# Attention with routed experts on one Trainium2 core: softmax weights as the stationary operand, row sums from a column of ones beside v, x kept in f32

## The chip, the core and the metric

The kernel runs on one core of one Trainium2 chip. The metric is the device time of one execution in microseconds (us). The core has a matrix engine (PE, with its weight loads shown apart as PEld), a vector engine (DVE), an activation engine (ACT), a general engine (POOL, GpSimd), a queue engine that issues transfers (SP) and sixteen DMA engines. [...]

## The reference

Rotary attention over 8 batches of 8 heads, 576 positions, 64 values each, then a dense layer plus one of eight experts for each token:

```python
q_rot, k_rot = (rotate(q), rotate(k))
scores = scale * np.matmul(q_rot, k_rot.transpose(0, 1, 3, 2))
scores = scores - np.max(scores, axis=-1, keepdims=True)
attn = np.exp(scores)
attn = attn / (np.sum(attn, axis=-1, keepdims=True) + 1e-09)
return np.matmul(attn, v).astype(np.float32)
...
x = np.ascontiguousarray(attn_out.transpose(0, 2, 1, 3)).reshape(B * S, H * D)   # (4608, 512)
y_dense = np.maximum(x @ w1_dense, 0.0) @ w2_dense
logits = x @ w_gate
expert_idx = np.argmax(logits, axis=1)
gate_w = softmax(logits)[np.arange(N), expert_idx]
y_moe[mask] = gate_w[mask, None] * (np.maximum(x[mask] @ w1[e], 0.0) @ w2[e])    # for each expert e
return (y_dense + y_moe).astype(np.float32)
```

## The kernel before

**Layout.** Two heads at a time (a head pair; 4 pairs in a batch, 32 in all) share tiles. The 576 positions are 512 "main" ones and 64 "tail" ones. Positions stand four by four on the partitions (position 4p+j on partition p, block j), the tail positions on 64 partitions of a fifth block. Nine strips of 128 key positions cover both heads of a pair: 0 to 3 and 5 to 8 are the main strips of the two heads, strip 4 holds both tails.

**One head pair goes through these functions.** `stage_load` brings q and k (f32) by SP's queue into `qk`. `stage_rope` rotates them into `nat` in bf16 (on DVE for the first two pairs, then on POOL). `stage_transpose` turns `nat` into `qkT` by a DMA transpose on SP. `s1_block` multiplies q and k for one strip of queries, and DVE takes the negative row maximum from PSUM (`negm`). `shift_rows` turns the maxima on PE (`mps`), splits them into two bf16 rows (`mT`, ACT and DVE) and copies them by two small SP transfers into spare rows of `qkT`, so that the second pass of scores has the maximum already subtracted. `s2_strip` and `s2_tails` do that second pass with keys on the partitions and take the exponential on ACT into `pm` (main queries) and `pt` (tail queries), in fp16.

**The weighted sums.** `av_mm` multiplies with v, or with a block of ones, as the stationary operand and the probabilities as the moving one; the two heads write to the two halves of the PSUM partitions. `av_sums` gives the row sums of the main queries, repeated on 64 partitions (ACT takes their logarithm, `lz`), `av_tails` the sums and values of the tail queries, `av_main` the values of the main queries. ACT makes the reciprocal as exp(-ln), DVE multiplies into `xf`: values on partitions, tokens along the free axis, f32. After the fourth pair of a batch POOL casts `xf` to `xb` (bf16).

**Logits.** `logits_part` multiplies `xf` with the gate weights in f32 in four column groups of PE at once, ACT copies to `lT`, and `logits_sum` turns that and adds the four groups by a product with `sel` (made once on DVE by `make_sel`). `x_turn` turns `xb` into `natx` (tokens on partitions) by a DMA transpose on SP, and `x_store` writes it as bf16 to the DRAM tensor `xd`.

**V.** `stage_v` loads a batch's v on POOL's queue with a cast to fp16, into one of two buffers `v16`.

**The order of work** is written out by hand: a loop over rounds i (0 to 33) and steps t (0 to 8), which emits at each step one `s1_block` of pair i+2, one `s2_strip` of pair i, and the rest at fixed steps:

```python
if t == 1: av_sums(i - 1)
if t == 4: av_tails(i - 1)
if t == 6: av_main(i - 1)
if t == 2 and i + 1 < NP: shift_rows(i + 1)
if t == 2 and i + LA < NP: stage_rope(i + LA); stage_transpose(i + LA)     # LA = 4
```

At t = 5 come the loads of q or k for later pairs, v of the next batch (in rounds 1, 5, 9, ...) and the expert weights (POOL's queue, rounds 8 to 24). The logits of a batch come in round 5, 9, 13, ..., `x_turn` at the end of rounds 6, 10, ... and `x_store` at the end of rounds 7, 11, .... Each engine and each queue takes its entries strictly in this order. PSUM tiles rotate: two for `s1`, two for `s2` (shared by the second scores, `mps` and the logits), two for `av`.

**Experts.** While the last rounds run, the tokens of the first six batches are planned into tiles of 128 by expert (`gate_steps`, `rank_steps`, `plan_steps`). Then `fetch` gathers each tile's rows of `xd` on POOL's queue (`xg`) and turns them by a DMA transpose (`xs`); `dense_in`, `expert_in`, `expert_turn` and `out_tile` compute a tile, and POOL scatters it to the output.

Of the kernel before, what the change touches and what calls it, by code (L numbers as in the profile page):

```python
# [24 lines left out]
def kernel(  # L25
# [88 lines left out]
    ones = const_p.tile([P, 3, D], fp16)  # L114
    nc.gpsimd.memset(ones, 0.0)
    nc.gpsimd.memset(ones[:, 0, :], 1.0)
    nc.gpsimd.memset(ones[0:64, 1, :], 1.0)
    nc.gpsimd.memset(ones[64:128, 2, :], 1.0)

# [8 lines left out]
    VB = 2  # L130
    v16s = []
    for i in range(VB):
        t = const_p.tile([P, HP, 10, D], fp16, name=f"v16_{i}")
        v16s.append(t)


    GC = 32
    wg_sb = const_p.tile([P, DT, GC], f32)
    nc.gpsimd.memset(wg_sb, 0.0)

    def load_gate():
        nc.sync.dma_start(wg_sb[:, :, 0:E], moe_w_gate.rearrange("(dt p) e -> p dt e", p=P))

    sel = const_p.tile([P, E], f32)

    def make_sel():
        nc.vector.tensor_copy(sel, ident_f[:, 0:E])
        for dt in range(1, DT):
            nc.vector.tensor_tensor(sel, sel, ident_f[:, GC * dt:GC * dt + E], AL.add)

# [4 lines left out]
    XR = DG // 2  # L155
# [20 lines left out]
    def route_constants():  # L176
        nc.gpsimd.iota(first_i, pattern=[[0, 5], [-1, E]], base=E, channel_multiplier=0)
        nc.gpsimd.tensor_copy(first, first_i)
        nc.gpsimd.memset(first[TAIL:P, 4, :], 0.0)
# [15 lines left out]
        nc.gpsimd.iota(tt, pattern=[[S, B], [0, 1]], base=MAIN + 1, channel_multiplier=1)  # L195
# [7 lines left out]
    xb = route_p.tile([P, 5, DT, P], bf16)  # L203
    natx = route_p.tile([P, 5, DG], bf16)
    dram_p = ctx.enter_context(tc.tile_pool(name="xd", bufs=1, space=bass.MemoryType.DRAM))
    xd = dram_p.tile([N, XR], i32)
# [24 lines left out]
    def pad_tails():  # L231

        for t in v16s:
            nc.gpsimd.memset(t[64:128, :, 4, :], 0.0)
            nc.gpsimd.memset(t[0:64, :, 9, :], 0.0)
        nc.gpsimd.memset(xb[:, 4, :, TAIL:P], 0.0)
        nc.gpsimd.memset(lgs, 0.0)
# [17 lines left out]
    def stage_v(b):  # L255
        v16 = v16s[b % VB]
        for a, blk in ((0, 0), (1, 5)):
            heads = v[b, a::2]
            nc.gpsimd.dma_start(v16[:, :, blk:blk + 4, :].rearrange("p h j d -> p h (j d)"),
                                heads[:, 0:MAIN, :].rearrange("h (p j) d -> p h (j d)", j=4))  # L260
            nc.gpsimd.dma_start(v16[64 * a:64 * a + 64, :, blk + 4, :],
                                heads[:, MAIN:S, :].rearrange("h p d -> p h d"))

    def stage_rope(i):
# [4 lines left out]
        if i < 2:  # L269
            a, s = (ap.tile([P, 2, 9, D], bf16, tag="lz", bufs=2, name=n) for n in ("ra", "rb"))  # L270
        else:
            a, s = (early.tile([P, 2, 9, D], bf16, tag=n, bufs=1, name=n) for n in ("ra", "rb"))
# [56 lines left out]
    TAILS = [0, 1, 2, 3, 5, 6, 7, 8, 4]  # L329

    def s2_strip(i, s):
        if s == 0:
            state["pm", i] = ap.tile([P, 9, MAIN], fp16, tag="pm", bufs=2, name="pm")
            state["pt", i] = ap.tile([P, 9, TAIL], fp16, tag="pt", bufs=2, name="pt")
        ps = pp.tile([P, 512], f32, tag="s2", bufs=2, name="s2")
        s2_mm(i, ps, s, False)
        nc.scalar.activation(state["pm", i][:, s], ps, AF.Exp, scale=float(scale))  # L337

    def s2_tails(i, part):
        pt = state["pt", i]  # L340
        n0, n1 = ((0, 8), (8, 9))[part]
        ps = pp.tile([P, 8, TAIL], f32, tag="s2", bufs=2, name="s2")
        for n in range(n0, n1):
            s2_mm(i, ps[:, n - n0], TAILS[n], True)
        nc.scalar.activation(pt[:, n0:n1], ps[:, 0:n1 - n0], AF.Exp, scale=float(scale))

    def av_mm(i, out_ap, tail, sums):

        b, u = divmod(i, HP)
        v16 = v16s[b % VB][:, u]  # L350
        for n in range(5):
            for h in range(2):
                strip = 4 if n == 4 else 5 * h + n
                lhsT = ones[:, 1 + h if n == 4 else 0, :] if sums else v16[:, 5 * h + n, :]
                rhs = state["pt", i][:, TAILS.index(strip)] if tail else state["pm", i][:, strip]
                nc.tensor.matmul(out_ap[64 * h:64 * h + 64], lhsT=lhsT, rhs=rhs, start=(n == 0), stop=(n == 4))  # L356


    def av_sums(i):
        lz = ap.tile([P, S], f32, tag="lz", bufs=2, name="lz")  # L360
        pz = pp.tile([P, 512], f32, tag="av", bufs=2, name="pz")
        av_mm(i, pz, False, True)
        nc.scalar.activation(lz[:, 0:MAIN], pz, AF.Ln)
        state["lz", i] = lz

    def av_tails(i):
        b, hp = divmod(i, HP)
        lz = state.pop(("lz", i))
        px = pp.tile([P, 2, TAIL], f32, tag="av", bufs=2, name="pxt")
        av_mm(i, px[:, 0], True, True)  # L370
        av_mm(i, px[:, 1], True, False)
        nc.scalar.activation(lz[:, MAIN:S], px[:, 0], AF.Ln)
        rz = lz
        nc.scalar.activation(rz, lz, AF.Exp, scale=-1.0)
        if hp == 0:
            state["xf"] = ap.tile([P, DT, S], f32, tag="xf", bufs=2, name="xf")
        nc.vector.tensor_tensor(state["xf"][:, hp, MAIN:S], px[:, 1], rz[:, MAIN:S], AL.mult)  # L377
        state["rz", i] = rz

    def av_main(i):  # L380
        b, hp = divmod(i, HP)
        rz = state.pop(("rz", i))
# [508 lines left out]
```

## Time and profile before

| | |
|---|---|
| median of 3 runs | 591.67 us (591.58 to 594.78) |
| profiled execution | 592.52 us |
| its span, first to last instruction | 590.8 us |
| granted TensorE clock, mean | 0.953 |
| PE busy | 489.3 us (83%) |
| DVE busy | 348.4 us (59%) |
| ACT busy | 295.2 us (50%) |
| POOL busy | 381.8 us (65%) |
| DMA traffic | 83.43 MB, mean 141 GB/s |

Busy times are shares of the whole span, which has stages with different limits; the stages have to be read one by one. PE's matmuls are pipelined, so that their durations overlap: what one costs is read from the start of the next. In a row such as `L326 PE MATMUL s<-qkT`, L326 is the line of the kernel, `s<-qkT` the tile written and the tile read, and after a bar stand idle time and what ended it. "SPq" is SP's queue: the time that issuing a transfer took, not the transfer.

### The profile page before, as it was taken

The numbers are of one execution on the slowest core, as the hardware profiler recorded it, in microseconds if no ns is written. First come the engines' busy times: TensorE is split into PE (matmuls) and PEld (weight loads), VectorE is DVE, ScalarE is ACT, GpSimd is POOL, SyncE is SP. The second block draws the span as 40 slices with busy tenths as digits, with TensorE's granted clock in tenths as the row PEclk, the third lists the DMA queues.
The fourth block names the chain that finished last, engine by engine and source line by source line (L and its number), as shares of the span: only waits on it lengthen the run. The fifth ranks groups of instructions, "written<-read, shape, count | busy, mean of one in ns | idle before, by whom it ended". The sixth has DMA issues, their size and how long they took to land. (4 is left out here: it accounts for less than half of the span.)

```text
span 590.8 us, 10570 instructions
## 1 busy us (share of the span) xinstructions
PE 489.3 (83%) x3756; PEld 241.7 (41%) x3756; DVE 348.4 (59%) x634; ACT 295.2 (50%) x598; POOL 381.8 (65%) x313
## 2 busy tenths in 40 slices
PE   0359988987897987887997898857789999999995
PEld 0124444433444433443443444424245544444452
DVE  8987777763776755765585688692148422222332
ACT  3006776764675765664675677662223333333330
POOL 4996989969859958966966934005335555555423
PEclk9999999987999988988898999897799999999999
DMA  5698754989987997988989673983914565456510
GB/s 160 123 180 139 145 132 89 179 170 173 178 189 143 186 160 154 159 185 164 153 162 199 87 139 65 194 142 69 222 52 135 132 145 145 136 145 137 127 54 0
DMA packets 176833, 83.43 MB, mean 141 GB/s; under 512 B 137776, under 2 KB 172080, under 8 KB 176784
## 3 DMA queue, kind: packets, MB, share of 16 engines
q1 hardware_dynamic: 148976, 53.53, 44.0%
q0 software_dynamic: 27808, 29.24, 27.1%
q8 instruction: 31, 0.51, 0.4%
q14 instruction: 18, 0.15, 0.1%
HBM read 52.84 MB, written 15.99 MB: 116 GB/s over the span
## 5 line engine op out<-in xcount | busy, mean ns | idle before, releaser
L305 DVE TENSOR_REDUCE negm<-s 128x1 f32<-128x576 f32 x288 | 207.8, 748 | 79.4 <-PE s L303 69.8
L337 ACT ACTIVATE pm<-s 128x512 f16<-128x512 f32 x288 | 163.1, 594 | 91.7 <-PE s L326 90.0
L326 PE MATMUL s<-qkT 128*128 128x64 bf16 (+1 forms) x512 | 114.5, 296 | 42.2 <-DMA qkT<-mT 22.2
L303 PE MATMUL s<-qkT 128*128 128x288 bf16 x512 | 113.6, 307 | 32.5 <-DMA qkT<-nat 23.4
L275 POOL TENSOR_TENSOR ra<-qk,cosx 128x1152 bf16<-128x1152 f32 x30 | 78.8, 2626 | 30.4 <-DMA qk<-in_k_dram 29.8
L794 POOL DMA_INDIRECT out_dram<-y,put_i x43 | 42.8, 996 | 80.8 <-DVE y L793 57.6
L303 PEld LDWEIGHTS <-qkT 128*128 128x128 bf16 x512 | 41.6, 101 | 94.6 <-issue 57.6
L730 POOL DMA_INDIRECT xg<-xd,take_i x43 | 43.5, 1011 | 46.3 <-DVE off L583 33.5
L278 POOL TENSOR_TENSOR nat<-ra,rb 128x1152 bf16<-128x1152 bf16 x30 | 71.3, 2375 | 2.4
L793 DVE COPY y<-py 128x512 f32<-128x512 f32 x43 | 29.7, 690 | 51.8 <-PE py L791 25.6
L764 ACT ACTIVATE hd<-pd 128x512 bf16<-128x512 f32 (+2 forms) x48 | 26.5, 552 | 64.8 <-PE py L789 53.6
L326 PEld LDWEIGHTS <-qkT 128*128 128x128 bf16 x512 | 37.0, 99 | 53.1 <-issue 24.7
L774 ACT ACTIVATE hn<-pe,gp 128x512 bf16<-128x512 f32 x43 | 29.5, 686 | 55.0 <-PE pe L771 36.6
L356 PE MATMUL pz<-pm,ones 128*64 128x512 f16 x320 | 50.6, 456 | 3.7 <-DVE xf L377 3.7
L762 PE MATMUL pd<-xs,w1d 128*128 128x512 bf16 (+2 forms) x192 | 47.3, 380 | 7.5 <-DMA xs<-xg 7.3
L782 DVE COPY he<-tr 128x512 bf16<-128x512 bf16 x43 | 18.2, 423 | 54.6 <-PE tr L780 45.7
L771 PE MATMUL pe<-w1e,xs 128*128 x172 | 45.9, 390 | 1.0 <-issue 1.0
L789 PE MATMUL py<-w2d,hd 128*128 128x512 bf16 x172 | 44.1, 379 | 0.0
L791 PE MATMUL py<-w2e,he 128*128 x172 | 44.1, 379 | 0.0
L277 POOL TENSOR_TENSOR rb<-qk,sinx 128x576 bf16<-128x576 f32 x30 | 43.0, 1433 | 0.0
L356 PEld LDWEIGHTS <-ones 128*64 128x64 f16 x640 | 28.7, 119 | 34.8 <-issue 24.6
L389 POOL CAST xb<-xf 128x2048 bf16<-128x2048 f32 x8 | 15.1, 1890 | 42.7 <-DVE xf L385 42.7
(168 smaller groups left out, 605.4 us busy)
## 6 DMA issues: line engine op xcount, KB each, us to landing
qk<-in_q_dram SPq DMA_DIRECT2D x32, 256.0 KB
qk<-in_k_dram SPq DMA_DIRECT2D x32, 256.0 KB
v<-in_v_dram POOLq DMA_DIRECT2D x16, 256.0 KB
xd<-natx SPq DMA_DIRECT2D x8, 512.0 KB
w1e<-in_moe_w_dram POOLq DMA_DIRECT2D x8, 512.0 KB
w2e<-in_moe_w_dram POOLq DMA_DIRECT2D x8, 512.0 KB
qk<-in_q_dram SPq DMA_DIRECT2D x32, 32.0 KB
qk<-in_k_dram SPq DMA_DIRECT2D x32, 32.0 KB
```

Of the source, the lines that this page charges most:

```text
L275: eng.tensor_tensor(a, x, cx, AL.mult)
L278: eng.tensor_tensor(nat[:, :, :, 0:D], a, s, AL.add)
L303: nc.tensor.matmul(ps[:, c, 0:CH], lhsT=qT[:, t * P:(t + 1) * P], rhs=kT[:, k0 + c * CH:k0 + (c + 1) * CH], start=True, stop=True)
L305: nc.vector.tensor_reduce(state["negm", i][:, t:t + 1], ps[:, :, 0:CH], axis=AX.XY, op=AL.max, negate=True)
L326: nc.tensor.matmul(out_ap, lhsT=kT[:, s * P:(s + 1) * P], rhs=qT[:, qa if s < 4 else qb], start=True, stop=True)
L337: nc.scalar.activation(state["pm", i][:, s], ps, AF.Exp, scale=float(scale))
L356: nc.tensor.matmul(out_ap[64 * h:64 * h + 64], lhsT=lhsT, rhs=rhs, start=(n == 0), stop=(n == 4))
L730: nc.gpsimd.indirect_dma_start(out=xg[:, u, :], out_offset=None, in_=xd[0:rows, :], in_offset=bass.IndirectOffsetOnAxis(ap=take_i[:, t:t + ...
L762: nc.tensor.matmul(ps[:, 0:n], lhsT=w1d[:, dt, ft * P:(ft + 1) * P], rhs=xs[:, 0:n, dt, :], start=(dt == 0), stop=(dt == DT - 1))
L771: nc.tensor.matmul(ps, lhsT=xs[:, u, dt, :], rhs=w[:, 0, dt, :], start=(dt == 0), stop=(dt == DT - 1))
L789: nc.tensor.matmul(py, lhsT=hd[:, ft, u], rhs=w2d[:, ft, :], start=(ft == 0), stop=False)
L791: nc.tensor.matmul(py, lhsT=he[:, ft], rhs=w[:, 0, ft, :], start=False, stop=(ft == FT - 1))
```

## The change

The probabilities become the stationary operand: for each head and each block of 128 queries, five products with 128x128 blocks of `pm` as weights, and 64 columns of v with a column of ones beside them as the moving operand. The result has tokens on partitions, and its 65th column is the row sum. DVE takes a reciprocal of the sums and multiplies into `xn` (f32, tokens on partitions). The fifth block takes the last 128 positions, so that its first 64 rows repeat earlier ones and are masked out later. `xn` is stored to `xd` as f32 directly; the gathers cast to bf16. For the logits, PE turns `xn` block by block (f32, against an identity), ACT copies the result out, and f32 products with the gate weights follow, in spare columns of the `av` tile. V is loaded as f32 by SP's queue into one buffer `vf` and cast to fp16 by ACT, one pair at a time. `pm` and `pt` become one tile; the `ones` blocks, `sel`, `xf`, `xb`, `natx`, `lT` and their steps go. The PSUM tile `av` now is one tile of two banks.

```diff
-        t = const_p.tile([P, HP, 10, D], fp16, name=f"v16_{i}")
+        t = const_p.tile([P, HP, 10, VC], fp16, name=f"v16_{i}")        # VC = D + 2
...
-    xd = dram_p.tile([N, XR], i32)
+    xd = dram_p.tile([N, DG], f32)
...
     def stage_v(b):
-        v16 = v16s[b % VB]
-        for a, blk in ((0, 0), (1, 5)):
-            heads = v[b, a::2]
-            nc.gpsimd.dma_start(v16[:, :, blk:blk + 4, :].rearrange("p h j d -> p h (j d)"),
-                                heads[:, 0:MAIN, :].rearrange("h (p j) d -> p h (j d)", j=4))
-            nc.gpsimd.dma_start(v16[64 * a:64 * a + 64, :, blk + 4, :],
-                                heads[:, MAIN:S, :].rearrange("h p d -> p h d"))
+        nc.sync.dma_start(vf.rearrange("p u (a j) d -> p (u a) (j d)", a=2)[:, :, 0:4 * D],
+                          v[b, :, 0:MAIN, :].rearrange("h (p j) d -> p h (j d)", j=4))
+        for a in range(2):
+            nc.sync.dma_start(vf[64 * a:64 * a + 64, :, 5 * a + 4, :],
+                              v[b, a::2, MAIN:S, :].rearrange("h p d -> p h d"))
+
+    def cast_v(b, u):
+        nc.scalar.copy(v16s[b % VB][:, u, :, 0:D], vf[:, u])
...
-    def av_mm(i, out_ap, tail, sums):
...
+    def av_tile():
+        return pp.tile([P, 2, 512], f32, tag="av", bufs=1, name="av")
+
+    def av_head(i, h):
         b, u = divmod(i, HP)
+        if h == 0:
+            state["av"] = av_tile()
+        for x in range(5):
+            q0 = x * P if x < 4 else S - P
+            for n in range(5):
+                nc.tensor.matmul(state["av"][:, h, x * VC:x * VC + D + 1],
+                                 lhsT=state["pm", i][:, 4 * h + n if n < 4 else 8, q0:q0 + P],
+                                 rhs=v16s[b % VB][:, u, 5 * h + n, 0:D + 1], start=(n == 0), stop=(n == 4))
+
+    def av_scale(i):
...
+        nc.vector.reciprocal(rz, o[:, :, :, D:D + 1])
+        nc.vector.tensor_tensor(state["xn", b][:, :, hp * P:(hp + 1) * P].rearrange("p j (h d) -> p h j d", d=D),
+                                o[:, :, :, 0:D], rz.broadcast_to([P, 2, 5, D]), AL.mult)
+
+    def x_store(b):
+        r0 = b * S
+        xn = state["xn", b]
+        nc.sync.dma_start(xd[r0:r0 + MAIN, :].rearrange("(p j) c -> p j c", j=4), xn[:, 0:4, :])
+        nc.sync.dma_start(xd[r0 + MAIN:r0 + S, :], xn[P - TAIL:P, 4, :])
+
+    def x_turn(b, j):
+        ps = pp.tile([P, DT, P], f32, tag="s2", bufs=2, name="xps")
+        for dt in range(DT):
+            nc.tensor.transpose(ps[:, dt], state["xn", b][:, j, dt * P:(dt + 1) * P], ident_f)
+        xT = ap.tile([P, DT, P], f32, tag="xT", bufs=2, name="xT")
+        nc.scalar.copy(xT, ps)
+        state["xT", j] = xT
+
+    def x_logits(b, js):
+        for n, j in enumerate(js):
+            xT = state.pop(("xT", j))
             for dt in range(DT):
+                nc.tensor.matmul(state["av"][:, n, LG:LG + E], lhsT=xT[:, dt], rhs=wg_sb[:, dt, :],
+                                 start=(dt == 0), stop=(dt == DT - 1))
+        nc.vector.tensor_copy(lgs[:, 5 * b + js[0]:5 * b + js[0] + len(js), :], state["av"][:, 0:len(js), LG:LG + E])
...
                 if i == 1 and t == 1:
                     shift_rows(0)
+                    for u in range(HP):
+                        cast_v(0, u)
...
-        make_sel()
...
         for i in range(NP + 2):
-            b = (i - 5) // HP if i >= 5 and (i - 5) % HP == 0 else None
+            b, x = divmod(i - 5, HP)
+            js = () if b < 0 or i > NP else ((0, 1), (2,), (3,), (4,))[x]
...
                     if t == 1:
-                        av_sums(i - 1)
-                    if t == 4:
-                        av_tails(i - 1)
-                    if t == 6:
-                        av_main(i - 1)
+                        av_head(i - 1, 0)
+                    if t == 3:
+                        av_head(i - 1, 1)
+                    if t == 5:
+                        if js:
+                            x_logits(b, js)
+                        av_scale(i - 1)
+                    if t == 2:
+                        for j in js:
+                            x_turn(b, j)
+                    if t == 8 and i % HP == 0:
+                        x_store(i // HP - 1)
...
+                if t == 4 and 2 <= i <= NP - LA:
+                    cast_v((i + 2) // HP, (i + 2) % HP)
+                if t == 2 and i == NP - LA:
+                    cast_v(B - 1, HP - 1)
...
-        x_turn(B - 1)
-        x_store(B - 1)
+        state["av"] = av_tile()
+        for js in ((0, 1), (2, 3), (4,)):
+            for j in js:
+                x_turn(B - 1, j)
+            x_logits(B - 1, js)
...
-        xg = pool.tile([P, m, XR], i32, tag=f"xg{tag}", bufs=bufs, name="xg")
+        xg = pool.tile([P, m, DG], bf16, tag=f"xg{tag}", bufs=bufs, name="xg")
...
+    vf = early.tile([P, HP, 10, D], f32, name="vf")
```

129 lines of the change are left out of this document (24 added, 105 removed).

## The prediction

> **What bounds the kernel now.** I cut the span first, by the windows view, at the ends of rounds (a round is one value of i in the attention loop, one head pair; nine steps t in it). Columns: window, length, busy time of PE, weight loads, DVE, ACT, POOL, granted clock, DMA share, GB/s.
>
> ```profile
> span 590.8 us, 10570 instructions
> 0.00:51.88 51.88, 20.22 (x80) 8.55 (x81) 45.44 (x62) 11.28 (x21) 42.89 (x47) 1.00 0.71 147
> 51.88:132.12 80.24, 72.26 (x674) 36.55 (x674) 58.58 (x101) 57.96 (x123) 66.28 (x56) 0.98 0.75 144
> 132.12:317.70 185.58, 156.79 (x1401) 77.46 (x1401) 118.52 (x201) 118.36 (x249) 148.65 (x97) 0.94 0.94 169
> 317.70:362.93 45.23, 38.91 (x352) 19.38 (x351) 29.58 (x51) 29.55 (x63) 28.01 (x19) 0.92 0.67 115
> 362.93:394.50 31.57, 25.24 (x230) 11.70 (x230) 24.24 (x63) 22.19 (x48) 7.47 (x10) 0.95 1.03 165
> 394.50:425.60 31.10, 19.29 (x145) 10.74 (x145) 7.83 (x21) 7.49 (x18) 13.84 (x14) 0.78 0.59 137
> 425.60:590.80 165.20, 156.57 (x880) 77.33 (x878) 64.18 (x139) 48.39 (x81) 74.69 (x74) 0.99 0.43 110
> ```
>
> The rows are: setup with round 0; rounds 1 to 8; rounds 9 to 24 (four batches, while expert weights load); 25 to 28; 29 to 31; the plan and the first expert tiles; the expert stage. The last is PE's (156.57 of 165.20) and holds none of the changed arithmetic. So the attention rounds decide. Single rounds, same view:
>
> ```profile
> 89.40:101.20 11.80, 10.71 (x108) 5.75 (x107) 8.18 (x15) 7.88 (x17) 11.72 (x10) 1.00 0.29 63
> 101.20:110.61 9.41, 8.61 (x84) 4.37 (x82) 6.79 (x12) 7.21 (x16) 9.24 (x6) 1.00 1.02 174
> 132.12:150.19 18.07, 13.31 (x107) 6.32 (x106) 8.26 (x15) 8.10 (x17) 17.91 (x14) 0.81 1.23 183
> 201.51:210.72 9.21, 8.59 (x81) 4.36 (x81) 7.26 (x13) 7.11 (x16) 6.29 (x4) 1.00 1.12 184
> ```
>
> An undisturbed round takes 9.21, PE 8.59 of it; DVE 7.26 and ACT 7.11 follow closely. Once per batch a round carries the logits and takes 11.80 (the next 9.41). An undisturbed batch is 11.80 + 9.41 + 2 x 9.21 = 39.6 us; rounds 9 to 24 took 185.58 / 4 = 46.4. The missing 6.8 is shown by the waits view (us, times, longest) and by the timeline of the 18.07 round:
>
> ```profile
> PE s L326 <- DMA qkT<-mT: 22.2, 9, 4.0
> 127.66 1.69 SPq L316 DMA_DIRECT2D qkT<-mT  x2
> 129.46 8.62 SPq L287 DMA_TRANSPOSE qkT<-nat  x1
> 136.69 0.58 PE L326 MATMUL s<-qkT 128*128 128x512 bf16 x1 [3.99 <-DMA qkT<-mT]
> 138.11 2.34 PE L356 MATMUL pz<-pm,ones 128*64 128x512 f16 x10
> ```
>
> The two rows of maxima, issued at 127.66, land 9.0 us later behind SP's loads; PE waits 3.99 and then runs slow: ten products take 2.34, against 1.27 below. Transposes, too, hold SP 8.62 us.
>
> **The weighted sums.** The PE timeline of a clean round (start, us):
>
> ```profile
> 200.98 0.39 PE L326 MATMUL s<-qkT 128*128 128x64 bf16 x8 [0.16 <-ACT pm L337]
> 202.83 1.27 PE L356 MATMUL pz<-pm,ones 128*64 128x512 f16 x10
> 204.03 0.42 PE L303 MATMUL s<-qkT 128*128 128x288 bf16 x2
> 206.14 0.32 PE L356 MATMUL pxt<-pt,ones 128*64 128x64 f16 x10
> 206.56 0.42 PE L303 MATMUL s<-qkT 128*128 128x288 bf16 x2
> 207.68 1.27 PE L356 MATMUL px<-pm,v 128*64 128x512 f16 x10
> 208.88 0.42 PE L303 MATMUL s<-qkT 128*128 128x288 bf16 x2
> ```
>
> From start to the next line's start, sums, tails and main take 1.20 + 0.42 + 1.20 = 2.82. In their place stand 2 x 25 products of 65 columns, each with its own 128x128 weights. Nearest is the x8 row: 64 columns, own weights, (0.39 - 0.19 for the last one's latency) / 7 = 0.029 each. 50 of them: 1.45. PE gets 1.37 a round less (bounds in the rivals).
>
> **DVE and ACT.** Groups by form (count, busy us, mean ns):
>
> ```profile
> L305 DVE TENSOR_REDUCE negm<-s 128x1 f32<-128x576 f32 x288 | 207.8, 748 | 79.4 <-PE s L303 69.8 <-PE s L299 7.6
> L374 ACT ACTIVATE lz<-lz 128x576 f32<-128x576 f32 x32 | 21.8, 683 | 1.0
> L385 DVE TENSOR_TENSOR xf<-px,lz 128x512 f32<-128x512 f32 x32 | 21.8, 681 | 0.0
> L363 ACT ACTIVATE lz<-pz 128x512 f32<-128x512 f32 x32 | 19.1, 597 | 32.5 <-PE pz L356 32.5
> L377 DVE TENSOR_TENSOR xf<-pxt,lz 128x64 f32<-128x64 f32 x32 | 7.2, 224 | 26.2 <-ACT lz L374 26.2
> ```
>
> DVE loses 0.68 + 0.22 and gains a multiply of 640 values (0.224 + 576 x 1.02 ns = 0.81, the slope between its two rows) and a reciprocal of ten (about 0.22, as the 64-wide row): 7.4 a round. ACT loses 0.60 + 0.68 and a 64-wide step (taken as 0.22 like DVE's) and gains a cast of V (640 values, 0.74 by the same slope rule) and 1.25 copies xT (0.60 each): 7.1. Neither gets lighter, and both were near the pace. So the round lies between 9.21 - 1.37 = 7.84 (all gained) and 9.21 (none). I take the middle, 8.6: shorter product blocks let ACT and DVE run more evenly, but they stay as full.
>
> **Logits.** Removed: 11.80 + 9.41 - 2 x 9.21 = 2.8 a batch. Added: 20 f32 transposes and 20 f32 products of 8 columns, spread over four rounds.
>
> ```profile
> 147.45 0.95 PE L410 MATMUL lps<-sel,lT 128*128 128x8 f32 x8
> 148.34 0.28 PE L411 MATMUL lps<-sel,lT 128*64 128x8 f32 x2
> ```
>
> An f32 load with eight columns costs (148.34 - 147.45) / 8 = 0.11. The 20 products: 2.2. A transpose is not shown at this size: 0.11 if its load hides, 0.22 if not; 2.2 to 4.4. I take the low end, as every other load here hides. Of 4.4 us, PE's unused gain (1.37 - 0.6 per round, 3.0 a batch) covers most; 1.5 shows, at the step where two turns and the maxima take three PSUM buffers in a row that ACT must empty. An undisturbed batch: 4 x 8.6 + 1.5 = 36 (up to 38).
>
> **V's new path** is the one added wait that I charge in full. V goes f32 through SP's queue into one buffer vf, issued at step 5 of the first round of a batch, behind that round's transposes and qk loads; step 4 of the next round casts it on ACT. If it is late, every exponential behind the cast waits, hence PE's second scores. SP in round 1, and two windows with one kind of transfer each (qk loads; transposes):
>
> ```profile
> 55.79 1.66 SPq L316 DMA_DIRECT2D qkT<-mT  x2
> 57.55 3.73 SPq L287 DMA_TRANSPOSE qkT<-nat  x1
> 63.32 0.65 SPq L245 DMA_DIRECT2D qk<-in_q_dram  x1
> 1.00:14.00 13.00, 0.00 (x0) 0.00 (x0) 11.11 (x24) 5.41 (x9) 5.31 (x17) 1.00 0.67 182
> 339.00:348.00 9.00, 8.59 (x81) 4.37 (x81) 7.05 (x13) 6.91 (x16) 6.25 (x4) 1.00 0.76 139
> ```
>
> SP is free for V at 63.32 + 0.65 = 64.0; its next entry, the following round's maxima (two copies, 1.66), then stands behind V's three issues. Loads run at 182 / 0.67 = 272 GB/s, V's 1.18 MB take 4.3, so V is there at about 69. Round 2 starts at 51.88 + 9.2 = 61.1, its fourth step comes 4 us later, at 65.1. Wait 4, and 1 for the slow clock that follows (2.34 against 1.27 above): 5 per batch, seven batches. In rounds 9 to 24, where transposes hold SP for 5 to 9, I take 7, and 1 for what is left of the late maxima: 44 a batch. Bounds: 0, if SP is early, and the rival below.
>
> DMA work: the turned x went by transposes at 139 / 0.76 = 183 GB/s; 0.655 MB is 3.6 a batch, gone. Storing x as f32 adds 0.59 MB, 2.2. V keeps its bytes read. From 0.94 x 185.58 / 4 = 43.6 a batch, 42 is left, or 44 if V's doubled write counts: just under the 44 above, so DMA gives no more. POOL loses its casts and V's issues: work beside the path, for PE's waits are on maxima, not on rotated q and k. The single buffer for both heads' sums costs nothing: the multiply at step 5 frees it four steps before the next round's first product, and if DVE ran that late, it would be the pace anyway. The store of x keeps two issues on SP.
>
> **Ends.** Setup: DVE's sel goes, V and four casts come ahead of the first exponentials.
>
> ```profile
> 40.21 3.76 DVE L149 TENSOR_TENSOR sel<-sel,ident_f 128x8 f32<-128x8 f32 x3
> 44.83 0.64 PE L303 MATMUL s<-qkT 128*128 128x288 bf16 x2 [3.71 <-DVE negm L305]
> 413.05 3.74 SPq L603 DMA_TRANSPOSE natx<-xb  x1
> ```
>
> -4.0, and +4.5 (V's 4.3 ahead of the first maxima, casts 3.0, less what waited anyway): +0.5 (-3 to +4). Rounds 29 to 31: three times 1.37, little else: -3. First expert tiles: SP loses a 3.74 transpose ahead of their loads, PE gains the last batch's turns and products: -1.5 (-4 to +3). Expert stage: gathers read f32 rows, twice the bytes, at a DMA share of 0.43, under a PE that is full: 0 (-1 to +5).
>
> **The sum**, against the profiled execution (592.52 us, 1.7 outside its span): setup +0.5; rounds 1 to 4 (51.88 to 89.40) 4 x 8.6 + 5 = 39.4 for 37.5, +1.9; rounds 5 to 8 36 + 5 + 1 = 42 for 42.7, -0.7; rounds 9 to 24 4 x 44 = 176 for 185.6, -9.6; 25 to 28 42 for 45.2, -3.2; then -3, -1.5, 0. Together -15.6: 592.5 - 15.6 = 577 us. The median of the three runs is 591.67, 0.85 under the profiled one; I leave that out.
>
> **Rivals.**
> (a) V is in time and the stalls go: batches at 36, at 40 in rounds 9 to 24. Rounds 1 to 4 34.4, 5 to 8 37, 25 to 28 37: -3.1 - 5.7 - 25.6 - 8.2 - 4 = 546. For it: the late maxima stood behind x's transposes and stores on SP. Against: V now stands on that queue.
> (b) DVE and ACT hold the round at 9.21: 0.6 x 28 = 17 more, 594, no change. For it: 7.4 and 7.1 of a round. Against: ACT's and DVE's idle time lies inside PE's long blocks.
> (c) Slower: V behind SP's backlog. The maxima took 9.0 from issue to landing; V needs 9.0 + 4.3 = 13.3 where I gave it 5. It costs 8.3 more in three batches and, where 2 are charged already, 6.3 in four, 50 in all: up to 627, and less as far as SP keeps up. It turns the sign at 15.6 / 7 = 2.2 us a batch beyond my wait.
> (d) Weight loads do not hide under 65 columns. A load alone lasts about 0.1:
>
> ```profile
> L326 PEld LDWEIGHTS <-qkT 128*128 128x128 bf16 x512 | 37.0, 99 | 53.1 <-issue 24.7 <-DMA qkT<-mT 20.4
> ```
>
> 50 x 0.099 = 4.95 a round, 3.5 more than 1.45, 112 over 32 rounds: 689. Against it stands the x8 row, where the same loads come every 0.029. [...]
>
> **How the numbers follow.** Forecast 0.47 (own range 562 to 592), (a) 0.20, (b) 0.13, (c) 0.17, (d) 0.03. One per cent, 5.9 us, is about what a measurement tells from no change. Faster: 0.36 + 0.20 + 0.03 = 0.59; same: 0.08 + 0.08 + 0.02 = 0.18; slower: 0.03 + 0.02 + 0.15 + 0.03 = 0.23. The range 538 to 612 leaves out a quarter of (a), half of (c) and all of (d), some 0.17.
>
> **What would show it.** Right: PE's products come every 0.03 us; undisturbed rounds near 8.6; a wait of ACT on vf of 4 to 6 us in the second round of each batch; no PE wait on mT over 4. Wrong: products every 0.08 or more (d); no wait on vf (a); rounds at 9.2 with DVE or ACT never idle (b); waits on vf near 13 (c).

## The result, and the profile after

The changed kernel takes 615.9 us (median of 4 runs, 613.94 to 616.72), the kernel before, on the same chip, 591.62 (590.41 to 594.78): a ratio of 1.0397, 95% interval 1.035 to 1.0444. It is slower, where I forecast 577 us. A few executions are over 1.5% longer than the fastest of their kernel; the ratios leave them out, and where the profile is of one (the kernel without logits, the one with expert weights spread) at most its undisturbed rounds are read. The windows view of the changed kernel, cut at the same events as before (setup with round 0; rounds 1 to 8; 9 to 24; 25 to 28; 29 to 31; then up to the first copy of an expert output y, and the rest; then two single rounds; the last row is the stretch up to the first y in the kernel before):

```profile
0.00:50.80 50.80, 19.90 (x80) 8.21 (x81) 41.82 (x58) 13.69 (x25) 38.48 (x39) 1.00 0.68 160
50.80:139.12 88.32, 68.66 (x788) 46.87 (x788) 63.65 (x103) 53.73 (x109) 65.70 (x49) 0.92 0.70 158
139.12:331.82 192.70, 152.24 (x1696) 109.81 (x1696) 123.55 (x208) 113.88 (x229) 129.17 (x73) 0.91 0.80 173
331.82:373.82 42.00, 34.93 (x425) 25.74 (x425) 30.64 (x52) 28.70 (x59) 18.21 (x12) 1.00 0.48 117
373.82:405.70 31.88, 25.05 (x282) 18.34 (x282) 27.08 (x64) 19.78 (x41) 3.20 (x5) 0.89 0.89 166
405.70:453.10 47.40, 34.77 (x222) 25.46 (x222) 7.75 (x33) 9.29 (x21) 11.41 (x12) 0.64 0.57 92
453.10:613.80 160.70, 150.85 (x856) 74.64 (x855) 62.42 (x129) 48.41 (x80) 74.58 (x74) 0.99 0.56 111
50.80:60.06 9.26, 7.33 (x91) 4.79 (x91) 7.49 (x12) 5.97 (x13) 4.33 (x3) 1.00 0.72 149
363.77:373.82 10.05, 8.38 (x104) 6.10 (x104) 7.66 (x13) 7.42 (x16) 2.79 (x4) 1.00 0.13 14
...
394.50:431.20 36.70, 24.84 (x166) 13.14 (x166) 10.08 (x32) 8.30 (x20) 13.84 (x14) 0.77 0.58 129
```

Against before: setup -1.1; rounds 1 to 8 +8.1; 9 to 24 +7.1; 25 to 28 -3.2; 29 to 31 +0.3; from there to the first y +10.7 (47.40 for 36.70); the rest +1.1. Together +23.0. PE is busy for less time in rounds 9 to 24 (152.24 for 156.79), and the stretch is longer all the same. The two rows of single rounds are an undisturbed one without logits, 9.26 (before 9.21), and one with a block of logits, 10.05. In both PE, DVE and ACT each have over 1.5 us to spare.

Where the spare time lies is seen in the timeline of that first round (start, us; in brackets the idle time before it and who ended it):

```profile
51.97 0.95 PE L341 MATMUL av<-v,pm 128*128 128x65 f16 x25
52.75 0.41 PE L288 MATMUL s<-qkT 128*128 128x288 bf16 x2
55.63 1.42 DVE L290 TENSOR_REDUCE negm<-s 128x1 f32<-128x576 f32 x2 [0.51 <-PE s L284]
56.97 0.21 DVE L351 RECIPROCAL rz<-av 128x10 f32<-128x10 f32 x1
57.21 0.83 DVE L352 TENSOR_TENSOR xn<-av,rz 128x640 f32<-128x640 f32 x1
57.96 2.08 DVE L290 TENSOR_REDUCE negm<-s 128x1 f32<-128x576 f32 x3
58.76 0.41 PE L288 MATMUL s<-qkT 128*128 128x288 bf16 x2 [1.03 <-DVE negm L290]
```

The 25 products of the first head take 52.75 - 51.97 = 0.78; those of the second start at 54.27. While PE does the second head's, DVE runs out of maxima (0.51 idle ahead of 55.63). Late in the round DVE does reciprocal and scaling as one lump of 57.96 - 56.97 = 0.99, and PE, two score blocks ahead, has no buffer and stands 1.03. In the kernel before the two multiplies stood apart:

```profile
207.81 0.22 DVE L377 TENSOR_TENSOR xf<-pxt,lz 128x64 f32<-128x64 f32 x1 [0.73 <-ACT lz L374]
207.95 1.41 DVE L305 TENSOR_REDUCE negm<-s 128x1 f32<-128x576 f32 x2
209.28 0.68 DVE L385 TENSOR_TENSOR xf<-px,lz 128x512 f32<-128x512 f32 x1
```

The waits (us in total, times, longest; the first row is from the kernel before) and a batch's second round, by ACT and PE:

```profile
PE s L303 <- DVE negm L305: 8.9, 9, 3.7
...
PE s L288 <- DVE negm L290: 29.0, 31, 3.5
ACT v L245 <- DMA vf<-in_v_dram: 29.7, 7, 8.4
PE s L311 <- DMA qkT<-mT: 6.1, 3, 3.0
212.36 0.72 ACT L245 CAST v<-vf 128x640 f16<-128x640 f32 x1 [4.62 <-DMA vf<-in_v_dram]
213.63 0.59 PE L311 MATMUL s<-qkT 128*128 128x512 bf16 x1 [4.45 <-ACT pm L321]
```

PE's wait for DVE's maxima at the score products has gone from 8.9 us to 29.0. The cast waits 4.62 for V, and PE 4.45 for ACT, behind the exponential that is queued after the cast. The wait for the rows of maxima has gone from 22.2 to 6.1. Logits, in an undisturbed round, and their rows by group:

```profile
356.13 0.60 PE L365 MATMUL xps<-ident_f,xn 128*128 128x128 f32 x4
359.60 0.95 PE L376 MATMUL av<-wg_sb,xT 128*128 128x8 f32 x8
360.41 0.41 PE L288 MATMUL s<-qkT 128*128 128x288 bf16 x2
L376 PEld LDWEIGHTS av<-wg_sb,xT 128*128 128x128 f32 x320 | 43.8, 206 | 3.4 <-ACT xT L367 2.0
```

Four f32 products of a block stand as eight records and take 360.41 - 359.60 = 0.81, so 0.20 each. And the end of the attention stage, with the same group of gathers (POOL xg) of the kernel before in the last row:

```profile
419.73 7.03 SPq L693 DMA_TRANSPOSE xs<-xg  x4
426.86 0.53 SPq L359 DMA_DIRECT2D xd<-xn  x1
431.80 0.45 ACT L725 ACTIVATE hd<-pd 128x128 bf16<-128x128 f32 x2 [6.42 <-DMA xd<-xn]
432.56 0.94 POOL L690 DMA_INDIRECT xg<-xd,take_i  x1 [11.34 <-ACT hd L725]
...
411.32 0.97 POOL L730 DMA_INDIRECT xg<-xd,take_i  x1 [0.27 <-POOL xb L391]
```

Expert activations (hd) wait for the last store of xn (xd<-xn), which stands on SP behind the first tiles' transposes, and the gathers wait for hd: by the program's order of allocation, their tiles take over the SBUF of the attention stage. The second group of gathers starts at 432.56, 26.9 us after the last round's end; before, at 411.32, 16.8 after it.

### The profile page after: what moved, and what is told of

Its sections match the earlier page's. It is cut to its first block, busy times and chain, and to the rows that moved or that the text cites. A ratio compares the mean times of both kernels' runs of the same rounds, so it can differ in the third digit from the quotient of the medians.

```text
span 613.8 us, 11625 instructions
## 1 busy us (share of the span) xinstructions
PE 486.4 (79%) x4348; PEld 309.1 (50%) x4348; DVE 356.9 (58%) x645; ACT 287.5 (47%) x558; POOL 340.7 (56%) x262
## 3 DMA queue, kind: packets, MB, share of 16 engines
q1 hardware_dynamic: 140912, 62.45, 44.3%
## 5 line engine op out<-in xcount | busy, mean ns | idle before, releaser
L321 ACT ACTIVATE pm<-s 128x512 f16<-128x512 f32 x288 | 165.5, 596 | 115.4 <-PE s L311 89.6
L288 PE MATMUL s<-qkT 128*128 128x288 bf16 x512 | 116.2, 312 | 51.7 <-DVE negm L290 29.0
L288 PEld LDWEIGHTS <-qkT 128*128 128x128 bf16 x512 | 45.9, 107 | 115.7 <-issue 79.8
L341 PEld LDWEIGHTS <-pm 128*128 128x128 f16 x1600 | 64.1, 102 | 21.9 <-issue 10.0
L341 PE MATMUL av<-v,pm 128*128 128x65 f16 x1600 | 65.9, 200 | 2.4 <-DVE xn L352 2.4
L311 PEld LDWEIGHTS <-qkT 128*128 128x128 bf16 x512 | 39.9, 105 | 24.5 <-issue 7.9
L376 PEld LDWEIGHTS av<-wg_sb,xT 128*128 128x128 f32 x320 | 43.8, 206 | 3.4 <-ACT xT L367 2.0
```

What stands on the lines that cost most here:

```text
L288: nc.tensor.matmul(ps[:, c, 0:CH], lhsT=qT[:, t * P:(t + 1) * P], rhs=kT[:, k0 + c * CH:k0 + (c + 1) * CH], start=True, stop=True)
L311: nc.tensor.matmul(out_ap, lhsT=kT[:, s * P:(s + 1) * P], rhs=qT[:, qa if s < 4 else qb], start=True, stop=True)
L321: nc.scalar.activation(state["pm", i][:, ORDER.index(s), 0:MAIN], ps, AF.Exp, scale=float(scale))
L341: nc.tensor.matmul(state["av"][:, h, x * VC:x * VC + D + 1], lhsT=state["pm", i][:, 4 * h + n if n < 4 else 8, q0:q0 + P], rhs=v16s[b % VB ...
```

## The experiments

The theory: (1) a round is a chain of lumps, each of which starves the other engine, since two score buffers cover no more than one reduction; the change took a lump from PE and put one on DVE; (2) V's one buffer costs ACT's waits; (3) logits cost PE 0.81 a block, uncovered; (4) the attention stage's SBUF comes free late. The rivals are in the expectations. Ratios are to the kernel before, run on the same chip.

**V issued a round earlier** (on the changed kernel).

```
-  if i % HP == 1 and i // HP + 1 < B: stage_v(i // HP + 1)
+  if i % HP == 0 and i // HP + 1 < B: stage_v(i // HP + 1)
   (the fourth cast of a batch one round earlier)
```

> One edit on the changed kernel: the V loads of the next batch are issued one round earlier (at the first round of a batch in place of the second), and the fourth cast of the V tile moves from the second round of the next batch to its first, so that two rounds instead of one lie between the issue and the first cast. Theory A, V's wait costs what ACT waited: ACT's 29.7 us of waiting on the V transfers (7 times) go below 8 us, only the first V of the prologue being left, and of the 21 us that go, most reaches the span because ACT's strips hold PE there: 596 to 602 us against the changed kernel's 615.9. Rival B, the same lateness comes back elsewhere: the earlier V loads take their place in the queue from the q and k loads, the rope on GpSimd then waits longer for the k transfer (now 88.6 us in 14 waits) and the rows of maxima wait for their DMA again (PE's wait on them 22 us in the kernel before, 6 now): 610 to 616 us, with ACT's wait on V gone all the same.

603.62 us, ratio 1.0192 (1.0093 to 1.0292): 12 us less, between the two.

```profile
ACT v L245 <- DMA vf<-in_v_dram: 8.5, 1, 8.5
PE s L311 <- DMA qkT<-mT: 12.7, 8, 3.6
136.94:315.94 179.00, 146.11 (x1698) 106.21 (x1697) 123.12 (x208) 113.09 (x229) 129.68 (x73) 0.95 0.89 186
```

ACT's waits on V are gone but for the first. Rounds 9 to 24 take 179.0 for 192.7, with the DMA share up from 0.80 to 0.89, and the wait on the rows of maxima has doubled, to 12.7; rounds 25 to 28 have gone from 42.00 to 46.18. Theory A for the larger part, rival B for the rest.

**The last batch's stores ahead of the first gathers** (on the changed kernel).

```
                         av_scale(i - 1)
+                        if i == NP: x_store(B - 1)
```

> One edit on the changed kernel: the two stores of the last batch's normalised tokens are issued right after the last scaling, ahead of the gathers of the first expert tiles in SP's queue, in place of behind them. Theory A, the expert stage starts late because its tiles take the SBUF of the attention stage, and that comes free only when these stores have read it: the waits of ACT's hd copy and of DVE's gate maximum for the stores (6.4 and 4.3 us) shrink, the second group of gathers starts some 4 to 9 us sooner than 432.6, the stretch from the end of the last round to the first y copy falls from 47.4 to 38 to 43 us: 607 to 612 us. Rival B, the stretch is set by the last batch's turns and logits and by the gate and plan after them on DVE, or the stores put the first gathers back by as much as they win: within 1.5 us of 615.9.

613.54 us, ratio 1.0347 (1.0249 to 1.0446): not told apart from the changed kernel. The stores went out ahead of the transposes, but the second group of gathers still starts 23.7 us after the last round's end, for 26.9, and the stretch from the last round's end (408.13) to the first y (452.89) is 44.8 us for 47.4:

```profile
428.57 0.58 ACT L367 COPY xT<-xps 128x512 f32<-128x512 f32 x1 [4.04 <-PE xps L365]
431.81 0.94 POOL L692 DMA_INDIRECT xg<-xd,take_i  x1 [6.82 <-issue]
```

The last turned tokens (xT) are in the same SBUF, copied at 428.57 and read by the products after that. One holder was taken away, and the next ended almost as late.

**The scaling split by head** (on the changed kernel).

```
-  if t == 3: av_head(i - 1, 1)
-  if t == 5: x_logits(b, js); av_scale(i - 1)
+  if t == 3: av_scale(i - 1, 0)
+  if t == 4: av_head(i - 1, 1)
+  if t == 6: x_logits(b, js); av_scale(i - 1, 1)
```

> One edit on the changed kernel: the reciprocal and scaling of a round, one lump of 1.03 us on DVE at the sixth of its nine steps, is split by head: the first head's half goes to the fourth step, the second head's products to the fifth and its half to the seventh, with the logits products. The work is the same but for one more DVE instruction pair per round. Theory A, the round is held by DVE's lump: the maxima of the two following blocks come late, and with two score buffers PE stands until they are done (29.0 us of PE waiting for maxima at the score products, 31 times, against 8.9 before). Then that wait falls below 12 us, the bare round goes from 9.26 to 8.5 to 8.9 us, the undisturbed batch from 42.0 to 39.5 to 40.5, and 30 rounds by 0.6 us each less the rounds that wait for V: 599 to 606 us. Rival B, a round is as long as PE's own products and ACT's nine strips and casts need, and DVE's wait is only where the slack shows: the wait at the score products moves to another line, round and batch stay within 0.15 and 0.6 us: 612 to 618 us.

614.03 us, ratio 1.0379 (1.0293 to 1.0465), and a bare round of 9.10, 0.16 less, where rival B allowed 0.15: near enough rival B. But the round's timeline has a wait that the split brought in:

```profile
366.51 0.49 DVE L352 TENSOR_TENSOR xn<-av,rz 128x320 f32<-128x320 f32 x1
367.05 0.95 PE L341 MATMUL av<-v,pm 128*128 128x65 f16 x25 [0.79 <-DVE xn L352]
```

The second head's products wait until the first head's scaling has read the tile that both share.

**No turns and no logits** (on the changed kernel; the logits are zero).

```
   def x_turn(b, j):
+      return
   def x_logits(b, js):
+      return
```

> One edit on the changed kernel: the turns of the tokens and the logits products are left out, and the logits are zero (so every token goes to the first expert, and the expert stage's weights are read for that expert; the number of tiles stays). It measures what turns and f32 logits products show of. Theory A, all of PE's time for them shows: five blocks of products at 0.81 and twenty turns at 0.11 to 0.15 make 6.2 to 7 us a batch, of which the batch in undisturbed rounds gives back 42.0 - 4 x 9.26 = 5.0: batch 37.0, seven batches 35 us less whatever V leaves, and the boundary's 12 us of turns and logits of the last batch go too: 575 to 588 us. Rival B, they lie in idle time of PE that DVE's lump makes anyway: the batch keeps 39.5 or more and the time is 595 to 605 us. In both cases the bare round stays at 9.26 if DVE holds it.

598.38 and 609.29 us. Undisturbed rounds take 9.25 each, so theory A holds for the rounds, and a block of logits costs a round 10.05 - 9.26 = 0.79, with 0.81 of products in it. The time, 598.38, is in rival B's range: something else limits the batch.

**A bank of its own for each head** (on the kernel with V issued earlier).

```
-  pp.tile([P, 2, 512], f32, tag="av", bufs=1)
+  pp.tile([P, 512], f32, tag=f"av{h}", bufs=1)
   t == 3: scaling of head 0;  t == 4: products of head 1
   t == 5: logits, in head 0's bank;  t == 6: scaling of head 1
```

> On the kernel with V issued earlier (603.62 us, bare round 9.25, round with one block of logits 10.04). The split of the scaling by head left the round at 9.10 and 9.89, but there PE stood 0.79 us ahead of the second head's products for the first head's scaling, because both heads share one two-bank tile. Here each head has a bank and a tile of its own, the logits go into the first head's bank once that is read, a step before the second scaling. Theory A, DVE's lump holds the round and the shared tile had put a wait in place of it: with the wait gone the bare round falls to 8.4 to 8.8 us and the batch from 41.4 to 38 to 40: 585 to 595 us. Rival B, the round is set by PE's order of work (its weighted sums, turns and logits stand between the score products, and DVE and ACT starve for as long): round 9.1 to 9.2, batch 40.8 to 41.3, 600 to 604 us.

596.2 us, ratio 1.0046 (1.0009 to 1.0083). Windows of a bare round, of one with a block of logits, and of rounds 9 to 12:

```profile
51.63:59.92 8.29, 7.49 (x92) 4.64 (x91) 7.03 (x14) 5.99 (x13) 3.44 (x2) 1.00 0.78 225
215.83:225.08 9.25, 8.46 (x103) 5.97 (x103) 7.89 (x16) 7.40 (x16) 9.08 (x7) 1.00 0.88 157
131.90:180.09 48.19, 37.97 (x425) 26.48 (x424) 31.85 (x61) 28.56 (x58) 31.91 (x19) 0.89 0.87 179
PE s L311 <- DMA qkT<-mT: 21.1, 10, 5.8
```

The bare round falls by 0.96, from 9.25 to 8.29, and the round with a block of logits by 0.79, from 10.04 to 9.25, with the same products on PE and one more reciprocal and multiply on DVE: theory A, and more than it had. A bank for each head without the split was not run; in the changed kernel PE's products waited for the scaling only twice, 2.4 us in all, so that there was little for it to free. The time is just above what theory A gave, as the wait for the rows of maxima is back at 21.1 us, 13.6 of it in rounds 9 to 24; these take 176.7 us, for 179.0 with V earlier alone.

**One key block of five in the weighted sums** (V earlier; the sums of the last block alone).

```
-  for n in range(5):   ... start=(n == 0), stop=(n == 4)
+  for n in range(4, 5):   ... start=True, stop=True
```

> On the kernel with V issued earlier: of the five key blocks of a weighted sum only the last is multiplied, so 10 products of 50 a round; the sums and what follows are those of that block alone. DVE's and ACT's work is unchanged, PE's falls by 40 x 0.031 = 1.24 us a round. Theory A, PE's work between the score products shows in full: bare round 9.25 to 8.0 to 8.2 and with a block of logits 8.8 to 9.0, 565 to 575 us if the DMA lets it. Rival B, DVE (9 maxima at 0.75, the lump of 1.03, the mT row 0.28: 8.1 us) or ACT holds it: at most 0.4 us a round, 592 to 600 us.

587.76 us, ratio 0.9909 (0.9872 to 0.9947).

```profile
51.57:59.69 8.12, 6.37 (x52) 3.49 (x52) 7.30 (x12) 6.09 (x13) 2.63 (x2) 1.00 0.71 214
```

40 products of 0.031, 1.24 us, less on PE make the bare round 1.13 shorter (8.12 for 9.25): theory A for the round, while the time stays well above its 565 to 575. So PE's products and DVE's lump both count almost in full, in a round in which each of the two is busy for about four fifths (7.33 and 7.49 of 9.26 in the changed kernel).

**Logits in fp16** (V earlier).

```
-  xT = ap.tile([P, DT, P], f32, ...);   rhs=wg_sb[:, dt, :]
+  xT = ap.tile([P, DT, P], fp16, ...);  rhs=wg_h[:, dt, :]
```

> On the kernel with V issued earlier: the turned tokens and the gate's weights are fp16 in place of f32 for the logits products alone (the turns stay f32; a token whose two best logits are close may go to another expert). Theory A, the f32 products are what the logits cost: four products of a block take 0.81 us because each goes through PE twice and loads f32 weights in 0.19 us. In fp16 they take 0.12 to 0.15, a round with one block falls from 10.04 to 9.35 to 9.45, a batch by 5 x 0.68 = 3.4 us, the last batch's 20 products at the slow clock by some 5 us: 603.6 less 20 to 27 = 577 to 584 us. Rival B, the round with logits is longer because of the order (turn, copy, product, copy, scaling in a chain over three engines) and not for the products' length: round 9.9 to 10.1 and 598 to 603 us, the last batch's share alone.

606.91 us, ratio 1.0213 (1.0147 to 1.028); the round with logits 9.81 for 10.04.

```profile
180.05 0.24 PE L377 MATMUL av<-wg_h,xT 128*128 128x8 f16 x4
180.28 0.41 PE L289 MATMUL s<-qkT 128*128 128x288 bf16 x2
```

The block's products go from 0.81 to 0.23, 0.58 less, but the round gets only 0.23 shorter: neither theory's number (9.35 to 9.45, or 9.9 to 10.1). What is left, 9.81 - 9.25, would be the turns and the copy of the logits in front of DVE's lump, as rival B has it; no run shows that apart. The total says little of the price of f32, because the edit moved other things: POOL, which casts the gate's weights, waits 12.9 us for them in the setup, round 2 takes 16.34 (9.95 with V earlier alone), and PE waits 24.8 us for the rows of maxima in place of 12.7.

**No logits, V earlier.**

> On the kernel with V issued earlier: turns and logits products left out, the logits zero, so every token goes to the first expert. Without V issued earlier this left 603.8 us with batches of 45.6 to 48.8 us from the tenth round on, although its undisturbed rounds were 9.25. Theory A, that floor was V's lateness: with V earlier the batches fall to 37 to 40 us and the time to 572 to 582 us. Rival B, the floor is what the DMA engines move in a batch while the expert weights load (42 to 44 us of their time was the estimate ahead of the change): batches of 43 to 46 us from the tenth to the twenty-fourth round, and 588 to 600 us.

588.79 us, ratio 0.9952 (0.9918 to 0.9986). Rounds 9 to 12, rounds 25 to 28, and the wait:

```profile
131.69:176.99 45.30, 31.84 (x364) 20.03 (x364) 30.14 (x48) 25.76 (x53) 32.41 (x19) 0.92 0.88 195
307.46:349.91 42.45, 32.48 (x364) 20.53 (x364) 30.05 (x48) 25.77 (x53) 19.32 (x13) 0.92 0.49 119
PE s L312 <- DMA qkT<-mT: 28.2, 8, 5.5
```

Rival B by its numbers: three of four rounds take 9.25 to 10.3, the fourth 15 to 17, and the batch stays at 45.30 with PE busy for 31.84 (the three that follow: 43.5, 44.3 and 42.6). Its reason, full DMA engines while the expert weights load, does not follow: the second row is rounds 25 to 28, where no expert weights are issued before 347.44, and they take 42.45 at a DMA share of 0.49, with one round of 14.68. There SP issues V from 310.26 on, then the stores of xn, and right behind them, at 313.27, the rows of maxima; PE gets them at 320.37, after a wait of 3.08. So what stands ahead of the rows in their queue may matter more than the total that is moved; no run changed that order.

**V pair by pair** (two banks). One quarter of vf is loaded after the cast that frees it.

```
-  stage_v(i // HP + 1)                          # 1 MB, once a batch
+  stage_v((i + 2) // HP + 1, (i + 2) % HP)      # 256 KB, each round
```

> On the kernel with a bank for each head (596.2 us): V comes pair by pair, 256 KB at a time right after the cast that frees its quarter of the tile, in place of 1 MB once a batch. The kernel with two banks does 9.25 in an undisturbed round, yet the four rounds from the tenth on took 48.2, 45.0, 42.2 and 41.4 us, with one round of 12 to 17 us in each, in which PE stood for the rows of maxima from DMA (21 us in 10 waits). Theory A, that is the burst: V's 1 MB stands ahead of those rows in the DMA engines once a batch. Spread over four rounds it costs nothing there, the wait on the rows falls below 10 us, the four batches to 40 to 42 us: 584 to 590 us. Rival B, the DMA engines are simply full in this stretch (busy share 0.89 with expert weights, q and k in f32, V and the stores in f32), and the waits spread as the transfers do: batches 42 to 47 us, 592 to 598 us.

597.74 us, ratio 1.0124 (1.0048 to 1.0201): in rival B's range.

```profile
183.89:228.10 44.21, 36.88 (x426) 25.95 (x425) 31.75 (x61) 28.65 (x58) 35.06 (x21) 0.96 0.92 192
```

The same batch as ever at a DMA share of 0.92, and 29.2 us of waits for the rows of maxima in place of 21.1. So V's burst is not the cause. That it is the amount is not shown: the stores of xn (1.18 MB) still go out at once, and rounds 25 to 28, with hardly any expert weights to load, again take 42.64 at a share of 0.59.

**Turns and logits by feature block** (V by pair, two banks). After each pair its 128 features are turned for all five token blocks, and the products added up by DVE; the stores were meant to go first.

```
-  for dt in range(DT): transpose(ps[:, dt], xn[:, j, dt*P:...])
+  for j in range(j0, j1): transpose(ps[:, j - j0], xn[:, j, dt*P:...])
+  nc.vector.tensor_tensor(o, o, p, AL.add)
```

> On the kernel with V by pair and a bank for each head, two edits at the end of the attention stage: the last batch's stores are issued right after its last scaling, and turns and logits go by feature block (five turns and five f32 products after each pair, added up on DVE) in place of by token block after the batch, so that after the last pair 5 turns and 5 products are left in place of 20 and 20. Theory A, what holds the expert stage back is the SBUF of the attention stage: with the stores alone moved ahead, the second group of gathers still started when the last turned tokens had been read (431.8 against 432.6 us). With both gone, the stretch from the end of the last round to the first y copy falls from 47.4 to 36 to 40 us, and the time by 8 to 11 us against V by pair alone. Rival B, the stretch follows the gathers and their transposes through SP (from the plan's end 37 us in the changed kernel, 28 in the one before): 44 to 47 us stay, and at most 3 us are won.

598.74 us, ratio 1.0152 (1.0061 to 1.0243). From the last round's end (391.68) to the first y (435.26): 43.6, rival B's number, but not for its reason. My edit had left the stores a step too late, behind the first transposes, and hd waits for them; the second group of gathers starts at 414.69:

```profile
408.99 0.53 SPq L358 DMA_DIRECT2D xd<-xn  x1
413.93 0.45 ACT L729 ACTIVATE hd<-pd 128x128 bf16<-128x128 f32 x2 [12.19 <-DMA xd<-xn]
```

**The same, with the stores really first.**

```
-  if t == 6: av_scale(i - 1, 1)
+  if t == (6 if i < NP else 5): av_scale(i - 1, 1); if i == NP: x_store(B - 1)
```

> On the kernel with turns and logits by feature block (598.74 us): there the last batch's stores, meant to go first, still stood behind the first four gathers' transposes in SP's queue (409.0 us, the transposes from 402.4 on), and the second group of gathers started at 414.7. Here the last scaling is one step earlier and its stores come ahead of the first gathers. So both things that hold the attention stage's SBUF end early, the stores and the last turned tokens (turned and multiplied by 403.5). Theory A, that SBUF is what the expert stage waits for: the second group of gathers starts right behind the first (404 to 406), the stretch from the end of the last round to the first y copy falls from 43.6 to 33 to 36 us, and the time to 589 to 592 us. Rival B, the stretch is set by the gathers and transposes themselves, or the stores delay the first gathers: 42 to 44 us, 596 to 600 us.

586.38 us, ratio 0.9899 (0.985 to 0.9949): about 1% less than the kernel before.

```profile
400.51 0.52 SPq L359 DMA_DIRECT2D xd<-xn  x1
407.94 0.94 POOL L693 DMA_INDIRECT xg<-xd,take_i  x1 [0.30 <-issue]
395.74:428.20 32.46, 20.66 (x178) 14.16 (x180) 6.27 (x28) 7.19 (x19) 11.45 (x12) 0.75 0.80 134
```

The second group of gathers (407.94) follows the first without a gap, and the stretch to the first y is 32.5 us, for 47.4 in the changed kernel and 36.7 in the one before: theory A, a little below its range.

**Expert weights spread over more rounds** (on that kernel).

```
-  if i % 2 == 0 and 10 <= i < 10 + 2 * E: load_w(...)
+  if i % 3 == 0 and 6 <= i < 6 + 3 * E: load_w(...)
```

> The same kernel as the one with the stores ahead of the first gathers, and one edit: the eight loads of expert weights go out every third round from the seventh on, in place of every second from the eleventh on. Theory A, from the tenth to the twenty-fifth round the DMA engines are full (busy share 0.88 to 0.93, batches of 40.8 to 44.0 us, against 0.53 and 40.2 in the batch without such loads): with 1.3 loads a batch for 2, the four batches come down to 39.5 to 41.5 and the time falls by 4 to 10 us against the kernel without this edit. Rival B, the waits for the rows of maxima come from single collisions and move with the loads to other rounds: the time stays within 2 us.

589.83 us, ratio 0.9941 (0.9906 to 0.9975), whose interval overlaps that of the kernel without the edit: no gain shown, as rival B has it. This, too, speaks against the amount as what holds these rounds.

## Why the prediction was wrong

**The price of the weighted sums held.** 25 products take 0.78, 0.031 each (I had 0.029 from the x8 row). Rival (d) falls with that: its 0.099 a load would have made 4.95 a round, where 50 products at the measured pace make 1.56. No run shows the 0.08 a product that I named as the sign of (d); the timeline shows 0.031.

**The round of 8.6 failed first.** I took the middle between 7.84 and 9.21 from busy sums and because "shorter product blocks let ACT and DVE run more evenly"; it came out at 9.26. The sums were right (DVE 7.49, forecast 7.4), but I did not ask when DVE's work falls due. Before, 0.22 and 0.68 stood apart, with maxima between them; now 0.99 comes at once, behind both heads' products. The gain was there (the cut products: 1.13 of 1.24 shows) and was given back on DVE (two banks: 0.96). Rival (b) had the right number for the round, but neither engine is full: it is the order within the round. By the sum's own terms this is 31 x 0.66 = 20 us, half of the 38.9 missed. As time the runs show less of it: two banks, with rounds shorter by 0.8 to 0.96, took the span from 602.4 to 593.7, and part of the rest went into waits for the rows of maxima.

**Logits: the price and the cover.** The term "20 products x 0.11" came from the row of eight records, which were four products, each recorded twice: 0.20 each, 4.05 a batch for 2.2. A load for these products lasts 206 ns in f32 and 97 in the kernel with fp16 logits; no run shows why. Turns lay within the bounds (0.60 for four, 3 a batch; I had 2.2 to 4.4, and took 2.2). The cover that I named, PE's unused gain, wasn't there, so an undisturbed batch showed 42.0 - 4 x 9.26 = 5.0 where I had 1.5, and took 42 for 36.

**V's wait held in kind.** In round 2 ACT waited 4.02 us, forecast 4. In rounds 9 to 24 it waited 3.6 to 4.6 a batch where I had taken 7, in round 6 1.0, and 8.4 in the setup; the wait on maxima fell from 22.2 to 6.1 as I had it. One round earlier gives 12 us back: 13.7 in rounds 9 to 24, while rounds 25 to 28 get 4.2 longer. In rounds 25 to 28 of the changed kernel V didn't wait at all, which set off the longer batch there: the 42 for that stretch came true for the wrong reason.

**The DMA floor: the number came out, the reason is not shown.** 42 to 44 a batch was forecast from the share of 0.94, and set beside V's 44 as if the two covered each other. Without logits, with two banks and with V by pair, rounds 9 to 24 take 43.9, 44.2 and 43.9 a batch on the mean (41 to 48 singly), whatever the round is worth. But rounds 25 to 28 of the same kernels take 42.5, 43.5 and 42.6 at DMA shares of 0.49 to 0.59. Their long rounds begin with a wait for the rows of maxima; why these land late, for the amount or for their place in the queue, stays open.

**Ends.** Setup: -1.1 for +0.5, within its bounds. Rounds 29 to 31: +0.3 for -3, cause open. First expert tiles: +10.7 for -1.5, outside the bounds of -4 to +3. I had counted the transpose that SP loses, and not asked who reads the attention stage's SBUF last. Before, the stored tokens lay in a tile that no expert tile reuses; now xn and xT lie where expert tiles follow, and both end late: the turns and products of the last batch run at a granted clock of 0.64. The kernels with turns by feature block show it: with the stores late the stretch to the first y was 43.6, with both in time 32.5, 11.1 less; the stores alone had brought 2.6. The expert stage: +1.1 for 0.

By stage, measured less forecast: setup -1.6, rounds 1 to 8 +6.9, 9 to 24 +16.7, 25 to 28 0, 29 to 31 +3.3, first tiles +12.2, expert stage +1.1: 38.6 of 38.9. A batch in rounds 9 to 24 took 48.2 for 44: 42.0 for 36 without waits, and 6.2 for 8 of waits. Some 2 us in rounds 1 to 8 have nothing to do with these terms: a cast on DVE in round 4 (2.41 us for 0.28, last section).

## What to carry to other kernels

A round on engines that are each four fifths busy need not be set by the fullest of them; here the lumps that each put into a chain with two buffers set it (8.29 for 9.25 with two banks). So, before you price work moved from one engine to another, mark where in the round it falls due, and give each part a bank of its own. At the end of a stage, list the last readers of the memory that the next stage takes over, and move all of them; moving one shows little (44.8 us for 47.4 with the stores alone, 32.5 with both). And a shorter round is worth little in a stretch where the next wait is for a transfer (with two banks rounds 9 to 24 took 176.7 us for 179.0).

## What the runs showed of the hardware

Each f32 product of the logits (128x128 weights, 8 columns) stands as two records, with 206 ns for a load, and takes 0.20 us; in fp16 products with 65 columns and weights of their own follow each other every 0.031. With V as 1 MB once a batch rounds 9 to 24 took 176.7 us, with V as 256 KB each round 175.6 (two banks in both; DMA share 0.87 and 0.92 in the batch shown of each). The DVE cast `parts<-pi` (128x80, int32 to bf16) took 0.28 us in the kernel before, where POOL was idle, and 2.41 in the changed one, where it began 0.08 after a POOL sum of 2.35; in seven other kernels it took 1.34 to 1.40. What sets its length no run shows. Between the stages the granted clock was 0.64 (0.77 in the kernel before, 0.75 in the fastest). The last 20 f32 products and their turns took 427.57 - 415.19 = 12.4 us there, where five blocks in undisturbed rounds are worth 5 x (0.81 + 0.60) = 7.0; part of the difference are waits for ACT's copies (0.29 and 0.73):

```profile
415.19 1.71 PE L365 MATMUL xps<-ident_f,xn 128*128 128x128 f32 x8
427.57 1.01 PE L723 MATMUL pd<-xs,w1d 128*128 128x128 bf16 x8 [0.26 <-DVE lgs L378]
```
